# Softmax attention beside linear attention on one core: shifted patterns by 64-bit integer additions on GpSimd, two small steps moved to VectorE

## The chip, the core and the metric

The kernel runs on one core of a Trainium2 chip. A core has TensorE (PE, matrix products into PSUM), VectorE (DVE), ScalarE (ACT) and GpSimd (POOL), each with its own instruction queue, and SyncE (SP), which here issues nearly all transfers. The metric is the device time of one execution in microseconds (us).

## The reference

Two attention blocks with their own inputs are computed and put side by side. Both have 2048 rows, width 512, 32 heads of 16 columns. A is linear attention; B is full softmax attention and holds nearly all of the work: 32 heads x 2048 x 2048 exponentials.

```python
# A: phi = lambda t: where(t > 0, t + 1, exp(t)) + 1e-6
#    o = phi(q) @ (phi(k)^T v) / (phi(q) . sum(phi(k)) + 1e-6);  a = o @ wo
# B:
scores = jnp.einsum("bhqd,bhkd->bhqk", q, k) * Dh ** -0.5
p = _softmax(scores, axis=-1)
o = jnp.einsum("bhqk,bhkd->bhqd", p, v)
b = o.transpose(0, 2, 1, 3).reshape(B, S, D) @ wo
return jnp.concatenate([a, b], axis=-1)
```

## The kernel before

**Blocks and units.** B's scores are cut into blocks of 128 keys x 512 queries of one head. Four heads of 32 rows each sit side by side in TensorE, so up to four blocks of scores (line 888) are made at once. There are 4 groups of 8 heads, 4 chunks of 512 queries and 2 halves of a group: 32 units of 64 blocks, 2048 blocks in all. No maximum is subtracted from the scores; a check of the sums at the end (FLG) decides whether a second, general program has to run, which it does not with these inputs.

**Two ways to an exponential.** Each block goes one of two ways.
- By ScalarE (line 1118): a "fill" of two or three blocks in a score region of PSUM (pS) is turned into PT by one activation, and each block is then multiplied with V once (line 1252).
- By VectorE and GpSimd: VectorE adds a constant to the scaled scores, caps them and writes them as 16-bit integers (DI, line 995). Read as float16, these bits are a coarse exponential. Two further patterns with the bits shifted by 341 and 683 (DJ, line 1191) are multiplied with copies of V scaled by 0.797 and 0.633 (VV, line 688), so that each such block takes three products with V in place of one. Up to four blocks form a group, whose DI buffer is 2048 columns wide, and each group gets its two patterns from one instruction each. There are 4 DI buffers and 6 DJ buffers.

Before the change a pattern is made by GpSimd with a tensor-scalar operation, or by VectorE when the planner finds GpSimd too far behind. GpSimd also makes the scaled copies of V for the head groups 1 to 3 (`v4_job`, lane "pool"; group 0 has them made by VectorE) and the division of B's rows by their sums (`unit_done`, line 1386; for the last unit `last_half`, line 1318): after the 64 blocks of a unit VectorE transposes the sums (OT), takes the reciprocal (ZRA), a product gives XN, and VectorE transposes XN into ON for the output projection.

**The order of the work.** The kernel writes every engine's instruction list out at build time. A planner simulates the engines with prices for each operation and picks, step by step, what comes next on which engine: fills, blocks of the second way, products with V, and jobs (projections, A's work, outputs). `SEEDS` holds one number for each 10 us of plan, which selects the planner's knobs (how much VectorE and GpSimd backlog is allowed, when VectorE takes a pattern) and a jitter on the jobs' due times. Blocks go the second way when the planned backlog of VectorE and of GpSimd is under a limit and a PSUM bank and a DI buffer are free. `POOLT` is the planner's price of a pattern on GpSimd, `XNT` that of a division. On the chip the engines follow these lists and wait for one another by semaphores.

A mark of kind "x" and `sch.hold` belong to VectorE operations that the planner lets run without GpSimd beside them: the plan starts such an operation behind GpSimd's running one, and the next GpSimd operation gets a semaphore wait for it. VectorE itself has no such wait.

**The start.** GpSimd writes the identity (identb, lines 425 and 426), on which 36 warming products on TensorE wait (line 1406), then the band masks, zeros in KM and ones in VV. TensorE's queue has the warming ahead of the first projections (line 580).

Of the kernel before, what the change touches and what calls it, by code (L numbers as in the profile page):

```python
# [3 lines left out]

# [2 lines left out]

BF = mybir.dt.bfloat16
F32 = mybir.dt.float32
F16 = mybir.dt.float16  # L10
I16 = mybir.dt.int16
U16 = mybir.dt.uint16
ACTF = mybir.ActivationFunctionType
ALU = mybir.AluOpType
AX = mybir.AxisListType
# [232 lines left out]
def bass_concat_heads__linear_attn_block__softmax_full_mha__prompt_kernel(nc, A_x, A_wqkv, A_wo, B_x, B_wqkv, B_wo, out):  # L248
# [26 lines left out]
    ALAG = 30.0  # L275
    SHL = ("pool", "pool")
    FU = 0.6
    SEEDS = (1060, 1060, 1468, 1468, 770, 905, 67, 2167, 165, 1387, 732, 509, 735, 1818, 1305, 1496, 450, 274, 1430, 603,
             940, 1969, 374, 709, 1904, 1001, 1158, 1423, 702, 411, 2124, 1060, 1060, 2149, 2149, 2149, 915, 1328, 1148, 329,
             1858, 405, 2177, 2129, 1827, 1827, 1827, 1214, 840, 675, 1266, 623, 1055, 1942, 1575, 119, 1711, 1454, 1454, 2031,  # L280
             2031, 1300, 4, 425, 392, 1368, 92)
    SEG = 10.0
    JIT = 6.0
    DBAL = 1
# [4 lines left out]
    LDA = 1  # L289
    JM = 0.8  # L290
    DSH = 0.45
    XNT = 0.63
    VVT = 0.69
    HINT = {"pe": 60, "act": 60, "dve": 150}
    FW = 3.4
# [1 line left out]
    AE = 40.0  # L297
    PH = 2
    NXA = 2
    XNP = 1  # L300
    VVP = 0
    POOLT = lambda w: 0.284 + w * 0.00082
    PACE = {"pe": 1.0, "act": 1.0, "dve": 1.03, "pool": 1.0, "dma": 1.0}
    TRACE = None

# [3 lines left out]
    SH = (0, 341, 683)  # L309
# [4 lines left out]
    sch = Sched()  # L314
    es = contextlib.ExitStack()
    with es:
# [18 lines left out]
        DI = sb("DI", [128, NDG, DG * 512], I16)  # L335
        DJ = sb("DJ", [128, NDJ, DG * 512], I16)
# [87 lines left out]
        def mk_ident(t, key):  # L424
            sch.add("pool", lambda e: e.memset(t[:], 0.0), writes=[key])
            sch.add("pool", lambda e: e.affine_select(out=t[:], in_=t[:], compare_op=ALU.not_equal, fill=1.0,
                                                      base=0, pattern=[[-1, 128]], channel_multiplier=1),
                    reads=[key], writes=[key])
        mk_ident(identb, "identb")
        sch.add("dve", lambda e: e.memset(DUM, 0.0), writes=["FLG"])  # L430
        sch.add("act", lambda e: e.activation(DUM[:, 4:8], DUM[:, 0:4], ACTF.Exp), reads=["FLG"], writes=["FLG"])
# [37 lines left out]
        def mode():  # L469
            return MODES[drawn[-1] % len(MODES)]  # L470
# [5 lines left out]
        def vis(eng, en_):  # L476
            return en_ + TAIL[eng] + SEM
# [66 lines left out]
        def f_op(lane, fn, reads=(), writes=()):  # L544
            return lambda bk: sch.add(lane, fn, reads=reads, writes=writes)
# [117 lines left out]
        def vcol(h):  # L663
            return VST * (h // 8) + 17 * (h % 8)

        def v4_job(t4, Gp, lane="pool", **kw):
            sl = Gp % 2
            def mm(e, bk, i):
                tl, cc = divmod(i, 4)
                t = 4 * t4 + tl  # L670
                return e.matmul(f32v(bk)[:, tl * 128:(tl + 1) * 128], lhsT=xTb[:, cc, t * 128:(t + 1) * 128],  # L671
                                rhs=Wb[:, cc, 1024 + Gp * 128:1024 + Gp * 128 + 128], start=(cc == 0), stop=(cc == 3))
            ts = range(4 * t4, 4 * t4 + 4)
            def load_wo():
                load(WOb, wob, [("Wb", 2)])
            st = halves(mm, [("Wb", 2)] + [("xTb", t) for t in ts], n=16, parts=NPP, dur=0.06, after=load_wo if (t4, Gp) == (3, NGP - 1) else None)
            vv = lambda k: VV[:, sl, k, 4 * t4:4 * t4 + 4, :].rearrange("p t c -> p (t c)")
            st.append(("dve", 0.6, f_ev("dve", lambda e, bk: e.tensor_copy(
                VV[:, sl, 0, 4 * t4:4 * t4 + 4, :].rearrange("p t (h c) -> p t h c", c=17)[:, :, :, 0:16],
                f32v(bk).rearrange("p (t h d) -> p t h d", t=4, d=16)), [], [("VV", t, sl, 0) for t in ts])))  # L680
            for k in (1, 2):
                if VVP == 1 and lane == "dve":
                    st.append(("dve", 0.6, f_ev("dve", lambda e, bk, k=k: e.tensor_scalar(
                        VV[:, sl, k, 4 * t4:4 * t4 + 4, :].rearrange("p t (h c) -> p t h c", c=17)[:, :, :, 0:16],
                        f32v(bk).rearrange("p (t h d) -> p t h d", t=4, d=16), SW[k], 0.0, op0=ALU.mult, op1=ALU.add),
                        [], [("VV", t, sl, k) for t in ts])))
                    continue
                cp = f_op(lane, lambda e, k=k: e.tensor_scalar(  # L688
                    vv(k), vv(0), SW[k], 0.0, op0=ALU.mult, op1=ALU.add),
                    [("VV", t, sl, 0) for t in ts] + [("VV1", sl)], [("VV", t, sl, k) for t in ts])  # L690
# [224 lines left out]
        pend = []  # L915
# [255 lines left out]
        def shift_cand():  # L1171
            if not pend:
                return None
            buf, k, n, w, I, items, t_ = pend[0]
            jb = jn[0] % NDJ
            if jfree[jb] is None:
                return None
            sp, sd = max(T["pool"], vis("dve", t_), jfree[jb]), max(T["dve"], t_, jfree[jb])
            dp, dd = POOLT(w), DSH + max(0.0, T["pool"] - sd)
            tp = sp + sum(c_[3] for c_ in cands["pool"]) + sum(POOLT(p_[3]) for p_ in pend)  # L1180
            td = sd + sum(c_[3] for c_ in cands["dve"]) + dd
            ln, st_, d_ = ("dve", sd, dd) if tp > td + mode()[5] else ("pool", sp, dp)
            def run(st_, en_):
                pend.pop(0)
                jn[0] += 1
                if ln == "dve":
                    T["pool"] = max(T["pool"], vis("dve", en_))
                jfree[jb] = None
                jleft[jb] = n
                J = DJ[:, jb, 0:w]  # L1190
                op = sch.add(ln, lambda e: e.tensor_scalar(J, I, 1.0, float(SH[k]), op0=ALU.mult, op1=ALU.add),  # L1191
                             reads=[("DI", buf, i) for i in range(n)], writes=[("DJ", jb)])
                if ln == "dve":
                    sch.hold.append(op)
                    op.x = DSH
                for i, b in enumerate(items):
                    pv_ready[b[0]].append((vis(ln, en_), b, k, DJ.bitcast(F16)[:, jb, i * 512:(i + 1) * 512], ("DJ", jb), ("j", jb)))
                free_di(buf, vis(ln, en_))
            return st_, 0.7 if ln == "pool" else 0, ln, d_, run, None, "f"
# [102 lines left out]
        def last_half(h, t_):  # L1302

            if h == 0:
# [7 lines left out]
            cs, bs = slice(256 * h, 256 * h + 256), slice(8 * h, 8 * h + 8)  # L1312
            ot, zk, xk = [("OT", 0) if h == 0 else ("OT", 9)], [("ZR", u) if h == 0 else ("ZR", u + 9)], [("XN", xb, 1) if h == 0 else ("XN", xb, 9)]
            src, skey = (PVb, [("PV", g) for g in range(4)]) if h == 0 else (f32v(lbank[0]), [lbank[0][3]])
            mlane = "pool"
            st = [("dve", 0.42, f_op("dve", lambda e: e.transpose(OT[:, 0, cs], src[:, 0:256]), skey, ot)),
                  ("dve", 0.2, f_op("dve", lambda e: e.reciprocal(zs, o[:, bs, 16]), ot, zk)),
                  (mlane, 0.44, f_op(mlane, lambda e: e.tensor_tensor(xn[:, bs, 16:32], o[:, bs, 0:16],
                                                                                  zs.unsqueeze(2).broadcast_to([128, 8, 16]), op=ALU.mult), ot + zk, xk)),
                  ("dve", 0.42, f_op("dve", lambda e: e.transpose(ON[:, k, cs], XN[:, xb, cs]), [("XN", xb, 0)] + xk, on_keys(k)[4 * h:4 * h + 4]))]  # L1320
            urgent.append(Job(st, [("ot", u - 1)], [(3, ("onf", h))] + ([(1, ("zr", u))] if h else []), bank=False, ready=t_, prio=0.5))
# [54 lines left out]
        def unit_done(u, t_):  # L1376
# [6 lines left out]
            o = OT[:, 0, :].rearrange("p (b r) -> p b r", r=32)  # L1383
            xn = XN[:, xb, :].rearrange("p (b r) -> p b r", r=32)
            zr = ZRA[:, 16 * u:16 * u + 16]
            mul = f_op("pool" if XNP else "dve", lambda e: e.tensor_tensor(xn[:, :, 16 * e_:16 * e_ + 16], o[:, :, 0:16],  # L1386
                                                        zr.unsqueeze(2).broadcast_to([128, 16, 16]), op=ALU.mult),
                       [("OT", 0), ("ZR", u)], [("XN", xb, e_)])
            def norm(bk):
                mul(bk)  # L1390
                give_back("OT", 0.0)
            st = [("dve", 0.26, f_op("dve", lambda e: e.reciprocal(zr, o[:, :, 16]), [("OT", 0)], [("ZR", u)])),
                  ("pool", XNT, norm) if XNP else ("dve", 0.96, norm)]
# [215 lines left out]
        def run(queue, e):  # L1609
            got, loc = [], []  # L1610
            def hook(e):
                e.wait_ge(sems["dve"], flag_op.count)
                got.append(e.value_load(FLG.bitcast(mybir.dt.int32), min_val=0))
            sch.emit_queue(queue, e, sems, hook=(flag_op.idx if queue == "pool" else len(sch.ops), hook),
# [57 lines left out]
```

## Time and profile before

| what | value |
|---|---|
| median of 3 runs | 668.36 us (667.43 to 670.56) |
| the profiled execution, first to last instruction | 665.0 us |
| ScalarE busy | 650.9 us (98%) |
| TensorE busy | 643.4 us (97%) |
| VectorE busy | 610.5 us (92%) |
| GpSimd busy | 584.9 us (88%) |

The profiled execution is listed by its span alone; the median of the runs stands 3.4 us above it. In the profile's lines, PEld is TensorE's weight load, "out<-in" names the tiles, "xN" is a count, and behind the bar stand the busy time, the mean of one in ns, and the idle time of the engine just before, with what ended it. Matmuls are pipelined, so a busy TensorE is not one at its peak.

### The profile page before, as it was taken

The numbers are of one execution on the slowest core, as the hardware profiler recorded it, in microseconds if no ns is written. First come the engines' busy times: TensorE is split into PE (matmuls) and PEld (weight loads), VectorE is DVE, ScalarE is ACT, GpSimd is POOL, SyncE is SP. The second block draws the span as 40 slices with busy tenths as digits, with TensorE's granted clock in tenths as the row PEclk, the third lists the DMA queues.
The fourth block names the chain that finished last, engine by engine and source line by source line (L and its number), as shares of the span: only waits on it lengthen the run. The fifth ranks groups of instructions, "written<-read, shape, count | busy, mean of one in ns | idle before, by whom it ended". The sixth has DMA issues, their size and how long they took to land.

```text
span 665.0 us, 19663 instructions
## 1 busy us (share of the span) xinstructions
PE 643.4 (97%) x8560; PEld 204.5 (31%) x8560; DVE 610.5 (92%) x995; ACT 650.9 (98%) x707; POOL 584.9 (88%) x367
## 2 busy tenths in 40 slices
PE   8999999999999999999999999999999999999998
PEld 4323322332333333333322223322223222223224
DVE  6999999899898999998889999999999999899994
ACT  5999999999999999999999999999999999999995
POOL 5788889889999899899998988988899988999883
PEclk9999999999999999999999999999999999999999
DMA  9500001201001010021101100110111011000102
GB/s 217 101 2 1 13 7 25 41 21 25 23 17 18 18 34 18 11 65 41 41 10 34 40 18 17 36 27 13 30 28 35 18 25 34 25 26 10 40 27 73
DMA packets 55414, 21.72 MB, mean 33 GB/s; under 512 B 45600, under 2 KB 55328, under 8 KB 55328
## 3 DMA queue, kind: packets, MB, share of 16 engines
q1 hardware_dynamic: 54128, 20.07, 13.1%
q8 instruction: 67, 1.10, 0.7%
q10 hardware_dynamic: 1200, 0.39, 0.2%
q14 instruction: 19, 0.16, 0.1%
HBM read 4.19 MB, written 4.19 MB: 13 GB/s over the span
## 4 chain that ended last, share of the span: by engine, by line
ACT 93%; PE 6%; DMA 1%; DVE 0%; issue 0%
ACT PT L1118 90%; PE pS L888 2%; ACT pD L708 1%; PE pPV L1252 1%; PE pD L551 1%; PE pS L551 1%; ACT pS L708 1%; DMA xTb<-in_B_x_dram 1%; PE pD L1252 0%; PE pS L580 0%; PE pD L580 0%; DVE KV L555 0%; PE pD L671 0%; PE pD L792 0%; DVE FLG L660 0%
## 5 line engine op out<-in xcount | busy, mean ns | idle before, releaser
L1118 ACT ACTIVATE PT<-pS 128x1024 f16<-128x1024 f32 (+1 forms) x668 | 643.3, 1346 | 1.9 <-PE pS L888 1.9
L1191 POOL TENSOR_SCALAR DJ<-DI 128x2048 int16<-128x2048 int16 (+1 forms) x287 | 543.8, 1895 | 62.6 <-DVE DJ L1191 31.9
L995 DVE TENSOR_SCALAR DI<-pD 128x512 uint16<-128x512 f32 (+1 forms) x464 | 317.7, 701 | 20.2 <-PE pD L888 15.9
L888 PE MATMUL pS<-QT,KM 32*128 32x512 bf16 x1566 | 261.8, 385 | 16.4 <-ACT PT L1118 12.2
L1252 PE MATMUL pPV<-PT,VV 128*17 128x512 f16 (+1 forms) x1381 | 226.4, 378 | 0.0
L1252 PE MATMUL pPV<-DJ,VV 128*17 128x512 f16 (+1 forms) x1334 | 218.1, 379 | 0.0
L888 PE MATMUL pD<-QT,KM 32*128 32x512 bf16 x482 | 172.2, 385 | 0.2 <-DVE DI L995 0.2
L888 PEld LDWEIGHTS pS<-QT,KM 32*128 32x128 bf16 x1566 | 64.6, 91 | 284.5 <-ACT PT L1118 261.1
L1252 PE MATMUL pPV<-DI,VV 128*17 128x512 f16 (+1 forms) x667 | 151.5, 379 | 0.0
L995 DVE TENSOR_SCALAR DI<-pS 128x512 uint16<-128x512 f32 x185 | 126.2, 682 | 5.0 <-PE pS L888 2.4
L1252 PEld LDWEIGHTS pPV<-PT,VV 128*17 128x17 bf16 x1381 | 45.8, 88 | 38.3 <-issue 35.7
L1252 PEld LDWEIGHTS pPV<-DJ,VV 128*17 128x17 bf16 x1334 | 44.3, 88 | 43.1 <-issue 37.8
L888 PEld LDWEIGHTS pD<-QT,KM 32*128 32x128 bf16 x482 | 40.8, 91 | 3.6 <-DVE DI L995 2.0
L1191 DVE TENSOR_SCALAR DJ<-DI 128x2048 int16<-128x2048 int16 x47 | 38.9, 830 | 0.1
L1252 PEld LDWEIGHTS pPV<-DI,VV 128*17 128x17 bf16 x667 | 31.6, 88 | 21.7 <-issue 17.8
L551 PE MATMUL pD<-xTb,Wb 128*32 128x512 bf16 x352 | 27.5, 384 | 0.0
L551 PE MATMUL pD<-Wa,xTa 128*32 128x256 bf16 x640 | 23.8, 274 | 0.0
L1381 DVE STREAM_TRANSPOSE OT<-pPV 128x512 f32<-128x512 f32 x31 | 21.9, 706 | 0.7 <-PE pPV L1252 0.7
L1386 POOL TENSOR_TENSOR XN<-OT,ZRA 128x256 bf16<-128x256 f32 x31 | 19.2, 620 | 3.6 <-DVE DJ L1191 2.5
L708 ACT ACTIVATE pD<-pD 128x512 f32<-128x512 f32 x20 | 18.0, 898 | 0.0
L551 PEld LDWEIGHTS pD<-Wa,xTa 128*32 128x32 bf16 x640 | 14.5, 96 | 8.1 <-issue 6.3
L688 POOL TENSOR_SCALAR VV<-VV 128x544 bf16<-128x544 bf16 x24 | 15.4, 645 | 1.7 <-DVE DJ L1191 0.6
(113 smaller groups left out, 394.4 us busy)
## 6 DMA issues: line engine op xcount, KB each, us to landing
out_dram<-KV SPq DMA_DIRECT2D x31, 128.0 KB, 1.7
Wa<-in_A_wqkv_dram SPq DMA_DIRECT2D x3, 512.0 KB, 4.7
KM<-KR SPq DMA_DIRECT2D x96, 16.0 KB, 1.8
Wb<-in_B_wqkv_dram SPq DMA_DIRECT2D x2, 384.0 KB, 6.1
Wb<-in_B_wqkv_dram SPq DMA_DIRECT2D x1, 512.0 KB, 4.5
Wa<-in_A_wo_dram SPq DMA_DIRECT2D x1, 512.0 KB, 4.2
Wb<-in_B_wo_dram SPq DMA_DIRECT2D x1, 512.0 KB, 4.2
xTa<-in_A_x_dram SPq DMA_TRANSPOSE x24, 3.2
```

The lines of the kernel that those rows point to most:

```text
L551: ins = e.matmul(out[32 * g:32 * g + 32], lhsT=lhsT[:, 32 * g:32 * g + 32], rhs=rhs, start=start, stop=stop, tile_position=(0, 32 * g))
L688: cp = f_op(lane, lambda e, k=k: e.tensor_scalar(vv(k), vv(0), SW[k], 0.0, op0=ALU.mult, op1=ALU.add), [("VV", t, sl, 0) for t in ts] + [( ...
L708: ex = lambda bk: sch.add("act", lambda e: e.activation(x(bk), x(bk), ACTF.Exp), reads=[bk[3]], writes=[bk[3]])
L888: return e.matmul(dst, lhsT=KM[32 * g:32 * g + 32, Gp % 2, e_, j * 128:(j + 1) * 128], rhs=QT[32 * g:32 * g + 32, Gp % 2, c * 512:(c + 1) ...
L995: sch.add("dve", lambda e: e.tensor_scalar(DI.bitcast(U16)[:, buf, i * 512:(i + n) * 512], f32v(DBANK[bi], 512 * n), EB, IMAX, op0=ALU.add ...
L1118: sch.add("act", lambda e: e.activation(PT[:, row, c0:c0 + w], SCR[sl][:, 0:w], ACTF.Exp, scale=SC / ESC), reads=skeys(sl)[:len(bl)], writ ...
L1191: op = sch.add(ln, lambda e: e.tensor_scalar(J, I, 1.0, float(SH[k]), op0=ALU.mult, op1=ALU.add), reads=[("DI", buf, i) for i in range(n)] ...
L1252: sch.add("pe", lambda e: e.matmul(dst[32 * g:32 * g + 17, 0:n], lhsT=VV[:, Gp % 2, k, j, 17 * h:17 * h + 17], rhs=P[:, q0:q0 + n], start= ...
L1381: sch.add("dve", lambda e: e.transpose(OT[:, 0, :], PVb[:, 0:512]), reads=[("PV", g) for g in range(4)], writes=[("OT", 0)])
L1386: mul = f_op("pool" if XNP else "dve", lambda e: e.tensor_tensor(xn[:, :, 16 * e_:16 * e_ + 16], o[:, :, 0:16], zr.unsqueeze(2).broadcast_ ...
```

## The change

- GpSimd makes all patterns: four 16-bit integers at a time are read as one 64-bit word, to which the shift, repeated four times, is added (`int64_add`). VectorE makes none any more. The instruction belongs to another library of GpSimd, which is loaded ahead of the identity; the standard library is loaded again at the end, before GpSimd waits for FLG.
- The products for the division of B's rows and the scaled copies of V go to VectorE, marked as operations without GpSimd beside them.
- The planner's prices of a pattern and of a division are others, and its seeds are others, so the order of the whole kernel is written anew.

```diff
+U64 = mybir.dt.uint64
+INTLIB = library_config.all_libraries[1]
...
-    SEEDS = (1060, 1060, 1468, 1468, 770, 905, 67, 2167, 165, 1387, 732, 509, 735, 1818, 1305, 1496, 450, 274, 1430, 603,
...
+    SEEDS = (384, 384, 384, 384, 725, 644, 67, 1773, 1773, 1031, 1260, 17, 1633, 497, 506, 36, 450, 865, 865, 865, 1631,
...
-    XNT = 0.63
-    XNP = 1
+    XNP = 0
+    XNT = 0.42
-    POOLT = lambda w: 0.284 + w * 0.00082
+    POOLT = lambda w: 0.19 + w * 0.000425
...
+        sch.add("pool", lambda e: e.load_library(INTLIB), writes=["lib"])
         mk_ident(identb, "identb")
...
-        def v4_job(t4, Gp, lane="pool", **kw):
+        def v4_job(t4, Gp, lane="dve", **kw):
...
-            sp, sd = max(T["pool"], vis("dve", t_), jfree[jb]), max(T["dve"], t_, jfree[jb])
-            dp, dd = POOLT(w), DSH + max(0.0, T["pool"] - sd)
-            tp = sp + sum(c_[3] for c_ in cands["pool"]) + sum(POOLT(p_[3]) for p_ in pend)
-            td = sd + sum(c_[3] for c_ in cands["dve"]) + dd
-            ln, st_, d_ = ("dve", sd, dd) if tp > td + mode()[5] else ("pool", sp, dp)
+            sp = max(T["pool"], vis("dve", t_), jfree[jb])
+            dp = POOLT(w)
+            ln, st_, d_ = "pool", sp, dp
...
-                op = sch.add(ln, lambda e: e.tensor_scalar(J, I, 1.0, float(SH[k]), op0=ALU.mult, op1=ALU.add),
-                             reads=[("DI", buf, i) for i in range(n)], writes=[("DJ", jb)])
+                sch.add(ln, lambda e: e.int64_add(J.bitcast(U64), I.bitcast(U64), SH[k] * 0x0001000100010001),
+                        reads=[("DI", buf, i) for i in range(n)], writes=[("DJ", jb)])
...
-            mlane = "pool"
+            mlane = "dve"
...
-            mul = f_op("pool" if XNP else "dve", lambda e: e.tensor_tensor(xn[:, :, 16 * e_:16 * e_ + 16], o[:, :, 0:16],
+            mul = f_op("dve", lambda e: e.tensor_tensor(xn[:, :, 16 * e_:16 * e_ + 16], o[:, :, 0:16],
...
             def norm(bk):
-                mul(bk)
+                sch.hold.append(mul(bk))
                 give_back("OT", 0.0)
+            norm.kind = "x"
...
             def hook(e):
+                if queue == "pool":
+                    e.load_library(library_config.standard)
                 e.wait_ge(sems["dve"], flag_op.count)
```

More of the change, by code (lines that the diff above doesn't have):

```diff
@@ L5 @@
 import concourse.bass as bass
-from concourse import mybir
+from concourse import library_config, mybir
 BF = mybir.dt.bfloat16
@@ L277, in bass_concat_heads__linear_attn_block__softmax_full_mha__prompt_kernel @@
     FU = 0.6
-    SEEDS = (1060, 1060, 1468, 1468, 770, 905, 67, 2167, 165, 1387, 732, 509, 735, 1818, 1305, 1496, 450, 274, 1430, 603,
-             940, 1969, 374, 709, 1904, 1001, 1158, 1423, 702, 411, 2124, 1060, 1060, 2149, 2149, 2149, 915, 1328, 1148, 329,
-             1858, 405, 2177, 2129, 1827, 1827, 1827, 1214, 840, 675, 1266, 623, 1055, 1942, 1575, 119, 1711, 1454, 1454, 2031,
-             2031, 1300, 4, 425, 392, 1368, 92)
+    SEEDS = (384, 384, 384, 384, 725, 644, 67, 1773, 1773, 1031, 1260, 17, 1633, 497, 506, 36, 450, 865, 865, 865, 1631, 579, 441, 360, 395, 307, 1378, 1216, 818, 817, 835, 835, 1060, 1059, 1059, 2149, 864, 864, 864, 866, 1858, 531, 513, 513, 513, 513, 513, 2102, 1566, 1572, 1995, 623, 622, 1063, 1069, 1078, 1072, 1479, 577, 2031, 678, 584, 531, 513, 392, 1121, 1120)
     SEG = 10.0
@@ L1185, in run @@
                 jn[0] += 1
-                if ln == "dve":
-                    T["pool"] = max(T["pool"], vis("dve", en_))
                 jfree[jb] = None
@@ L1190, in run @@
                 J = DJ[:, jb, 0:w]
-                op = sch.add(ln, lambda e: e.tensor_scalar(J, I, 1.0, float(SH[k]), op0=ALU.mult, op1=ALU.add),
-                             reads=[("DI", buf, i) for i in range(n)], writes=[("DJ", jb)])
-                if ln == "dve":
-                    sch.hold.append(op)
-                    op.x = DSH
+                sch.add(ln, lambda e: e.int64_add(J.bitcast(U64), I.bitcast(U64), SH[k] * 0x0001000100010001),
+                        reads=[("DI", buf, i) for i in range(n)], writes=[("DJ", jb)])
                 for i, b in enumerate(items):
@@ L1314, in last_half @@
             src, skey = (PVb, [("PV", g) for g in range(4)]) if h == 0 else (f32v(lbank[0]), [lbank[0][3]])
-            mlane = "pool"
+            mlane = "dve"
             st = [("dve", 0.42, f_op("dve", lambda e: e.transpose(OT[:, 0, cs], src[:, 0:256]), skey, ot)),
                   ("dve", 0.2, f_op("dve", lambda e: e.reciprocal(zs, o[:, bs, 16]), ot, zk)),
-                  (mlane, 0.44, f_op(mlane, lambda e: e.tensor_tensor(xn[:, bs, 16:32], o[:, bs, 0:16],
+                  (mlane, 0.28, f_op(mlane, lambda e: e.tensor_tensor(xn[:, bs, 16:32], o[:, bs, 0:16],
                                                                                   zs.unsqueeze(2).broadcast_to([128, 8, 16]), op=ALU.mult), ot + zk, xk)),
@@ L1389, in norm @@
             def norm(bk):
-                mul(bk)
+                sch.hold.append(mul(bk))
                 give_back("OT", 0.0)
+            norm.kind = "x"
             st = [("dve", 0.26, f_op("dve", lambda e: e.reciprocal(zr, o[:, :, 16]), [("OT", 0)], [("ZR", u)])),
-                  ("pool", XNT, norm) if XNP else ("dve", 0.96, norm)]
+                  ("dve", XNT, norm)]
             if e_ == 1:
```

## The prediction

> **What bounds the kernel now.** I read the page first (busy shares, chain), then ScalarE's waits, then a table of the work by stretches of time, then the groups by line, and last the first and the final microseconds of the timeline.
>
> ```profile
> span 665.0 us, 19663 instructions
> PE 643.4 (97%) x8560; PEld 204.5 (31%) x8560; DVE 610.5 (92%) x995; ACT 650.9 (98%) x707; POOL 584.9 (88%) x367
> ACT 93%; PE 6%; DMA 1%; DVE 0%; issue 0%
> ...
> ACT PT L1118 <- PE pS L888: 1.9, 2, 1.6
> PEld pS L888 <- ACT PT L1118: 261.1, 579, 0.8
> ...
> 146.27 10.09 ACT PT L1118 x11
> ```
>
> ScalarE carries the chain (93%) and its exponentials wait for TensorE only 1.9 us. TensorE's 97% is mostly overlap: its score loads stood still 261.1 us until ScalarE freed a score region. The eleven fills of the piece at 146.27 come every 10.09 / 11 = 0.917 us; a fill is two blocks of 512 columns, so a block costs ScalarE 0.459 us. The time falls only if blocks leave ScalarE for the other path (VectorE's DI, GpSimd's DJ), or if what lies before or behind its unbroken run shrinks. Which engine limits that other path? The stretches tell (after start and length: PE, PEld, DVE, ACT, POOL busy).
>
> ```profile
> 0.00:10.00 10.00, 7.93 (x77) 5.63 (x77) 3.83 (x12) 3.12 (x5) 6.95 (x23) 1.00 0.91 197
> 10.00:60.00 50.00, 47.79 (x533) 15.05 (x530) 48.68 (x76) 49.72 (x54) 38.69 (x22) 1.00 0.31 67
> 310.00:360.00 50.00, 48.62 (x684) 16.44 (x672) 41.13 (x66) 50.00 (x55) 47.92 (x29) 1.00 0.14 35
> 360.00:410.00 50.00, 49.09 (x625) 15.25 (x625) 49.08 (x81) 50.00 (x57) 43.91 (x28) 1.00 0.11 25
> 560.00:610.00 50.00, 49.44 (x681) 14.47 (x675) 45.54 (x76) 50.00 (x56) 48.12 (x28) 1.00 0.07 23
> ...
> 10.00:640.00 630.00, 613.96 (x8094) 188.73 (x8091) 590.69 (x953) 629.72 (x685) 566.10 (x335) 1.00 0.13 29
> ```
>
> From 10 to 640 us ScalarE works 629.72 of 630. VectorE works 590.69 (93.8%), and where GpSimd is fullest (47.92, 48.12) VectorE has least (41.13, 45.54); where GpSimd has room (38.69, 43.91) VectorE reaches 48.68 and 49.08 of 50, which is 97.4 and 98.2%. So GpSimd's patterns hold the second path back, and VectorE is next behind it. What the two engines do there:
>
> ```profile
> L995 DVE TENSOR_SCALAR DI<-pD 128x512 uint16<-128x512 f32 (+1 forms) x464 | 317.7, 701 | 20.2 <-PE pD L888 15.9
> L995 DVE TENSOR_SCALAR DI<-pS 128x512 uint16<-128x512 f32 x185 | 126.2, 682 | 5.0 <-PE pS L888 2.4
> L888 PE MATMUL pS<-QT,KM 32*128 32x512 bf16 x1566 | 261.8, 385 | 16.4 <-ACT PT L1118 12.2
> L888 PE MATMUL pD<-QT,KM 32*128 32x512 bf16 x482 | 172.2, 385 | 0.2 <-DVE DI L995 0.2
> ...
> L1191 POOL TENSOR_SCALAR DJ<-DI x287: 1471/1897/1901, 13.6 to 651.7; 128x2048 int16<-128x2048 int16 x143, 128x1536 int16<-128x1536 int16 x1
> L1191 DVE TENSOR_SCALAR DJ<-DI x47: 649/711/1848, 44.7 to 644.2; 128x2048 int16<-128x2048 int16 x47
> L1191 DVE TENSOR_SCALAR DJ<-DI 128x2048 int16<-128x2048 int16 x45 | 36.4, 811 | 0.1
> ...
> POOL DJ L1191 <- DVE DJ L1191: 31.9, 40, 1.5
> ```
>
> Of 1566 + 482 = 2048 blocks, 482 + 185 = 667 go the second way, at (317.7 + 126.2) / 667 = 0.666 us of VectorE each. Their patterns (DJ) are 287 on GpSimd at 1.897 us and 47 on VectorE, 36.4 us of them between 10 and 640; GpSimd stood still 31.9 us for those 47.
>
> **The change, part by part.** *The patterns.* A 64-bit add over 2048 int16 columns is 512 words of 64 bits, or 1024 of 32. No row shows this instruction. GpSimd's two tensor-scalar rows give its rate:
>
> ```profile
> L1191 POOL TENSOR_SCALAR DJ<-DI 128x2048 int16<-128x2048 int16 x285 | 540.8, 1898 | 62.5 <-DVE DJ L1191 31.9 <-DVE DI L995 8.7 <-DVE VV L688 3.3
> L688 POOL TENSOR_SCALAR VV<-VV 128x544 bf16<-128x544 bf16 x24 | 15.4, 645 | 1.7 <-DVE DJ L1191 0.6
> L688 DVE TENSOR_SCALAR VV<-VV x8: 283/901/1786, 14.0 to 35.7; 128x544 bf16<-128x544 bf16 x8
> L688 DVE TENSOR_SCALAR VV<-VV 128x544 bf16<-128x544 bf16 x8 | 7.7, 966 | 0.0
> ```
>
> (1898 - 645) / (2048 - 544) = 0.833 ns an element and 192 ns fixed. If one step handles 32 bits, a pattern takes 192 + 1024 x 0.833 = 1045 ns (my estimate). Bounds: one step for 64 bits gives 619 ns; a step for each 16 bits, or two for each 32-bit half, gives the old 1898. I take 1045, since 32-bit operands are the widest that any row here shows on that engine. Some 345 patterns are then 361 us, 54% of the span: GpSimd stops being a limit, and its 80 us of old idle time and holds cost nothing any more.
>
> *VectorE's account, 10 to 640 us.* It loses the 45 patterns: -36.4. It gains 24 copies of V, uncontended 283 ns (the minimum above): +6.8. It gains 30 of the 31 row divisions (L1386, one starts at 642.9), a product of two tensors over 256 columns, for which the neighbours are:
>
> ```profile
> L1386 POOL TENSOR_TENSOR XN<-OT,ZRA x31: 617/619/624, 39.7 to 642.9; 128x256 bf16<-128x256 f32 x31
> L761 DVE TENSOR_TENSOR RHA<-pD,BMk 128x128 bf16<-128x128 f32 x4 | 1.1, 279 | 0.0
> L796 DVE TENSOR_TENSOR KV<-pD,RD 128x512 bf16<-128x512 f32 x11 | 7.5, 679 | 1.3 <-PE pD L792 1.3
> ```
>
> 279 + 128/384 x (679 - 279) = 412 ns, so +12.4. Both kinds have to get past a running GpSimd instruction: VectorE's V copies had a mean of 966 against 283 at best (683 ns of delay behind operations of 1898), its patterns 811 against 649 (162 ns). Scaled to 1045 ns that is 89 to 376 ns each, 4.8 to 20.3 us for 54. I take GpSimd's busy share times half an operation, 0.54 x 522 = 282 ns: +15.2. While VectorE waits so, its DI evictions queue behind, which is why it is charged in full; the next GpSimd pattern is held until the operation is done, which its 46% of idle time hides (without that cover, 54 x 0.4 = 22 us). Then VectorE may fill up: at 97.5%, between the two best stretches, 0.975 x 630 - 590.7 = +23.6 us. Room for blocks: 23.6 + 36.4 - 6.8 - 12.4 - 15.2 = 25.6 us.
>
> *What that room is worth.* Each moved block costs VectorE 0.666, saves ScalarE 0.459 and so shortens the stage, in which VectorE loses 0.975 x 0.459 = 0.448: n = 25.6 / (0.666 + 0.448) = 23 blocks, 23 x 0.459 = **-10.6 us**. Ends: no better filling and 20.3 of delay give 36.4 - 19.2 - 20.3 = -3.1, n = -3, **+1.3**; filling at 98.2% (+28.0) and 4.8 of delay give 40.4, n = 36, **-16.6**. TensorE gets two more V products a block, 46 of some 0.055 us (four run at once in 0.22), 2.5 us inside its 261 us of standing still. Late next: ScalarE's own rate again, with VectorE level beside it. The new seeds and prices of the planner only pick this order; I charge them nothing, with the ends above as their cover. SP's queue gets no new transfer and loses none.
>
> *The library at the start.* A load stands ahead of identb on GpSimd's queue, and 36 warming matmuls wait for identb ahead of the first projection on TensorE's:
>
> ```profile
> 0.80 0.20 POOL L425 MEMSET identb<- 128x128 bf16 x1 [0.29 <-POOLq L1657]
> 1.24 0.29 POOL L426 TENSOR_SCALAR_AFFINE_SELECT identb<-identb 128x128 bf16<-128x128 bf16 x1 [0.24 <-POOL identb L425]
> 1.59 4.02 PE L1406 MATMUL pD<-identb 128*128 128x128 bf16 x36 [1.59 <-POOL ZMk L443]
> 1.84 1.28 ACT L431 ACT_TABLE_LOAD   x1 [1.84 <-issue]
> 2.14 0.22 DVE L450 TENSOR_REDUCE PAR<-ZMk 128x1 f32<-128x4 f32 x2 [0.52 <-POOL ZMk L446]
> 5.87 0.40 PE L580 MATMUL pS<-xTb,Wb 128*128 128x128 bf16 x4 [0.26 <-DMA xTb<-in_B_x_dram]
> 6.30 0.35 DVE L584 TENSOR_SCALAR KM<-pS,PAR 128x128 bf16<-128x128 f32 x1 [3.94 <-PE pS L580]
> 8.76 7.91 ACT L1118 ACTIVATE PT<-pS 128x1024 f16<-128x1024 f32 x8 [1.64 <-PE pS L888]
> ...
> 0.81 5.01 DMA xTb<-in_B_x_dram
> ...
> Wb<-in_B_wqkv_dram SPq DMA_DIRECT2D x2, 384.0 KB, 6.1
> ```
>
> The warming ends at 1.59 + 4.02 = 5.61 and the first projection starts at 5.87: 0.26 us of slack. PAR has 6.30 - 2.36 = 3.94 of slack, the first exponential none. Every microsecond of load beyond 0.26 therefore moves TensorE's first work and the whole unbroken run of ScalarE. No load is in this trace. Nearest: an engine's table load, 1.28 us; the first transfer of xTb, 5.01, out of the same moment, when the DMA engines are 91% busy (first stretch above); the longest transfer, 6.1. From 0 (beside the work) to 5.8; a gain is excluded, nothing starts earlier for it. I take the transfer of the same moment: 5.0 - 0.26 = **+4.7 us**.
>
> The Trainium skill speaks against the change here: GPSIMD Engine Reference, section 2.1 Instruction dispatch, says that the first call into a freshly loaded kernel pays for fetching its code, about 6 us (5.95 measured there). No run here shows it yet; by that figure alone the start would lose 5.95 - 0.26 = 5.7 us and the sum below would be 663.2.
>
> *The end.* The last two divisions change engine, and the standard library is loaded before GpSimd waits for FLG.
>
> ```profile
> L1318 POOL TENSOR_TENSOR XN<-OT,ZRA 128x128 bf16<-128x128 f32 x2 | 0.8, 402 | 5.0 <-DVE ZRA L1317 5.0
> 658.17 0.76 POOL L1318 TENSOR_TENSOR XN<-OT,ZRA 128x128 bf16<-128x128 f32 x2 [5.00 <-DVE ZRA L1317]
> 662.68 0.27 DVE L660 TENSOR_REDUCE FLG<-pPV 1x1 f32<-1x128 f32 x1
> ```
>
> 402 becomes 279 ns, with one hand-over less each way: **-0.3** (0 to -0.6). GpSimd's last pattern ends at 651.7 + 1.9 = 653.6 and FLG at 662.95: 9.3 us cover the second load, which therefore costs nothing (at 12 us it would cost 3).
>
> Sum: -10.6 + 4.7 - 0.3 = -6.2, a span of 658.8. The span of 665.0 stands 3.4 below the median of the runs, 668.36; with the same 3.4, **662.2 us**.
>
> **The rivals.**
> *The load is hidden* (it runs beside the preamble, or is as short as the table load): 662.2 - 4.7 = 657.5. For it: 1.28 us for ScalarE's table. Against: the full DMA engines.
> *The load is long*, twice the longest transfer: +11.9 instead of +4.7, 669.4, no change. For it: nothing but that the trace has no price.
> *VectorE does not fill up*, the rival on the other side: its idle time was TensorE's lateness (20.2 us before DI, 15.9 of it for pD), not GpSimd's fullness, and stays at 93.8%. Room 25.6 - 23.6 = 2.0, n = 2, -0.8; with the start +3.6: 672.0, slower. It decides from a filling below 95.1%, where n = 9.6 blocks just pay the load. Against it: the stretches with 97.4 and 98.2%.
> *The integer add is not faster than the old pattern*: 345 x 1.898 = 655 us on GpSimd, with 18 before its first pattern and 11 behind its last 684, so 687. It decides from (659 - 29) / 345 = 1.83 us. For it: nothing measured; against: the rate per element above.
>
> **How the numbers follow.** Forecast (662.2, its own range 656 to 667) 0.5; load hidden 0.2; load long 0.1; VectorE does not fill 0.15; slow add 0.05. Half a per cent (3.3 us) is about what a measurement of this kernel can tell from no change. Faster: 0.42 of the forecast's half and the 0.2, 0.62. Same: 0.08 of the forecast, 0.07 of the long load, 0.06 of the unfilled VectorE, 0.21. Slower: 0.09, 0.03 and the 0.05, 0.17. The range runs from the best end of the blocks with half the load hidden (668.4 - 16.6 - 0.3 + 2.3 = 654, and a little below for a load hidden whole, 652) to the unfilled VectorE (672); about 0.2 lies outside.
>
> **What would show it.** Patterns on L1191's successor near 1.05 us and GpSimd near 54 to 60% busy; VectorE at 97% or more from 10 to 640; about 690 blocks on the second path and 1358 on ScalarE; divisions at 0.41 us and V copies at 0.28 plus delay; identb ready near 6 us and the first exponential near 13.5 instead of 8.76. The prediction is wrong if the first exponential stays near 9, if VectorE remains near 94% with TensorE named before its DI, or if patterns near 1.8 us chain GpSimd.

## The result: slower, with not one block moved

The changed kernel takes 678.2 us (678.0 to 679.1, four runs) against 668.8 us before: ratio 1.0143, interval 1.0125 to 1.0161. The forecast was 662.2. The profiled execution spans 676.4 us, 11.4 more than the 665.0 before. Each listed time stands some 1.8 us above the span of its run (678.16 and 676.4 here), so the 665.0 belongs to an execution of about 666.8 (my estimate), 2 us below the median before; that is why the spans differ by 11.4 and the medians by 9.4. First the page of the changed kernel (busy times, chain, and the groups that answer to those of before):

```profile
span 676.4 us, 19637 instructions
PE 647.6 (96%) x8561; PEld 204.9 (30%) x8561; DVE 605.4 (90%) x1015; ACT 651.5 (96%) x707; POOL 350.5 (52%) x359
ACT 89%; PE 8%; issue 1%; DVE 1%; POOL 0%; POOLq 0%; DVEq 0%
...
L1187 POOL INT64_ADD DJ<-DI x336 | 343.5, 1034 | 305.8 <-DVE DI L995 270.0
L995 DVE TENSOR_SCALAR DI<-pD 128x512 uint16<-128x512 f32 (+1 forms) x472 | 318.9, 691 | 28.4 <-PE pD L888 21.6
L888 PE MATMUL pS<-QT,KM 32*128 32x512 bf16 x1568 | 261.5, 385 | 16.7 <-ACT PT L1118 11.7
...
L888 PE MATMUL pD<-QT,KM 32*128 32x512 bf16 x480 | 173.2, 385 | 0.0
...
L995 DVE TENSOR_SCALAR DI<-pS 128x512 uint16<-128x512 f32 x187 | 127.6, 682 | 7.5 <-PE pS L888 5.5
```

A pattern takes 1034 ns in place of 1898, and GpSimd fell from 88 to 52% busy, waiting 270 us for VectorE's DI. But 480 + 187 = 667 blocks go the second way, as many as before. ScalarE has the same 1381 blocks and the same busy time (651.5 against 650.9), and now also waits. The start, by the timeline:

```profile
8.17 0.19 POOL L424 MEMSET identb<- 128x128 bf16 x1 [7.66 <-issue]
8.52 0.29 POOL L425 TENSOR_SCALAR_AFFINE_SELECT identb<-identb 128x128 bf16<-128x128 bf16 x1 [0.16 <-POOL identb L424]
8.87 3.82 PE L1400 MATMUL pD<-identb 128*128 128x128 bf16 x36 [8.87 <-POOL ZMk L443]
12.53 0.39 PE L580 MATMUL pS<-xTb,Wb 128*128 128x128 bf16 x4
15.36 10.72 ACT L1118 ACTIVATE PT<-pS 128x1024 f16<-128x1024 f32 x11 [1.57 <-PE pS L888]
```

GpSimd stands still 7.66 us ahead of the identity (0.29 before), the 36 warming products start at 8.87 instead of 1.59, the first projection at 12.53 instead of 5.87, the first exponential at 15.36 instead of 8.76: +6.6 us. The last exponentials (line 1038, both kernels, before first) and ScalarE's waits in the changed kernel:

```profile
L1038 ACT ACTIVATE PT<-pS x2: 1103/1110/1117, 655.1 to 655.8; 128x768 f16<-128x768 f32 x2
```
```profile
L1038 ACT ACTIVATE PT<-pS x2: 1122/1123/1124, 667.8 to 668.5; 128x768 f16<-128x768 f32 x2
...
ACT PT L1118 <- PE pD L888: 2.9, 2, 2.5
ACT PT L1118 <- PE pS L888: 2.2, 2, 1.6
ACT pD L708 <- DVE PQT L707: 2.1, 1, 2.1
```

ScalarE's run from first to last exponential is 669.6 - 15.4 = 654.3 us against 656.9 - 8.8 = 648.2: +6.1, with equal work. Before, ScalarE waited for line 1118 only 1.9 us, 1.6 of it ahead of the first exponential. Now it waits 2.9 + 2.2 + 2.1, of which 1.6 is again ahead of the first: 5.6 us of holes inside the run (0.3 before), with two single ones of 2.5 and 2.1. Behind the last exponential stand 676.4 - 669.6 = 6.8 us against 8.1: -1.3. So 6.6 + 6.1 - 1.3 = 11.4.

The stretches of the changed kernel, for the same times as in the prediction, and last the long stretch of the kernel before:

```profile
310.00:360.00 50.00, 49.19 (x665) 14.66 (x667) 44.29 (x73) 50.00 (x55) 24.94 (x25) 1.00 0.07 15
360.00:410.00 50.00, 48.65 (x595) 14.77 (x591) 46.90 (x78) 50.00 (x55) 28.09 (x28) 1.00 0.11 26
560.00:610.00 50.00, 48.92 (x637) 13.54 (x625) 46.30 (x79) 50.00 (x56) 27.45 (x27) 1.00 0.06 18
...
60.00:640.00 580.00, 565.58 (x7489) 172.78 (x7486) 534.57 (x886) 577.22 (x628) 310.04 (x304) 1.00 0.12 25
```
```profile
60.00:640.00 580.00, 566.17 (x7564) 173.68 (x7561) 542.01 (x878) 580.00 (x633) 527.41 (x314) 1.00 0.11 26
```

With GpSimd about half idle in all of them, VectorE did not fill: 534.57 of 580 us, 92.2%, where the kernel before had 542.01 in the same stretch (93.4%).

### The profile page after: what moved, and what is told of

Same layout as the page of the kernel before. It is cut to its first block, busy times and chain, and to the rows that moved or that the text cites. A ratio compares the mean times of both kernels' runs of the same rounds, so it can differ in the third digit from the quotient of the medians.

```text
span 676.4 us, 19637 instructions
## 1 busy us (share of the span) xinstructions
PE 647.6 (96%) x8561; PEld 204.9 (30%) x8561; DVE 605.4 (90%) x1015; ACT 651.5 (96%) x707; POOL 350.5 (52%) x359
## 4 chain that ended last, share of the span: by engine, by line
ACT 89%; PE 8%; issue 1%; DVE 1%; POOL 0%; POOLq 0%; DVEq 0%
ACT PT L1118 87%; PE pS L888 3%; PE pPV L1245 2%; ACT pD L708 2%; PE pD L551 1%; ACT pS L708 1%; PE pD L1400 1%; PE pS L551 0%; DVE KV L555 0%; PE pD L671 0%; PE pS L671 0%; PE pD L580 0%; PE pS L580 0%; PE pPV L1497 0%; DVE OT L1309 0%
## 5 line engine op out<-in xcount | busy, mean ns | idle before, releaser
L1187 POOL INT64_ADD DJ<-DI x336 | 343.5, 1034 | 305.8 <-DVE DI L995 270.0
L995 DVE TENSOR_SCALAR DI<-pD 128x512 uint16<-128x512 f32 (+1 forms) x472 | 318.9, 691 | 28.4 <-PE pD L888 21.6
L888 PE MATMUL pS<-QT,KM 32*128 32x512 bf16 x1568 | 261.5, 385 | 16.7 <-ACT PT L1118 11.7
L1245 PE MATMUL pPV<-PT,VV 128*17 128x512 f16 (+1 forms) x1381 | 238.0, 379 | 0.0
L1245 PE MATMUL pPV<-DJ,VV 128*17 128x512 f16 (+1 forms) x1334 | 226.2, 380 | 0.0
L1245 PE MATMUL pPV<-DI,VV 128*17 128x512 f16 (+1 forms) x667 | 159.4, 382 | 0.0
L1245 PEld LDWEIGHTS pPV<-PT,VV 128*17 128x17 bf16 x1381 | 48.0, 88 | 44.3 <-issue 39.8
L1245 PEld LDWEIGHTS pPV<-DI,VV 128*17 128x17 bf16 x667 | 34.2, 88 | 21.7 <-issue 20.6
L551 PE MATMUL pD<-xTb,Wb 128*32 128x512 bf16 x288 | 21.7, 383 | 0.0
L1379 DVE TENSOR_TENSOR XN<-OT,ZRA 128x256 bf16<-128x256 f32 x31 | 20.4, 657 | 0.2
L555 DVE CAST KV<-pD 128x512 bf16<-128x512 f32 x19 | 13.0, 684 | 7.0 <-PE pD L551 7.0
L688 DVE TENSOR_SCALAR VV<-VV 128x544 bf16<-128x544 bf16 x32 | 15.8, 501 | 0.0
```

Source lines behind the costliest of these rows:

```text
L551: ins = e.matmul(out[32 * g:32 * g + 32], lhsT=lhsT[:, 32 * g:32 * g + 32], rhs=rhs, start=start, stop=stop, tile_position=(0, 32 * g))
L555: return lambda e, bk: (e.tensor_copy(out_fn(), in_fn(bk)) if lane == "dve" else e.activation(out_fn(), in_fn(bk), ACTF.Copy))
L688: cp = f_op(lane, lambda e, k=k: e.tensor_scalar(vv(k), vv(0), SW[k], 0.0, op0=ALU.mult, op1=ALU.add), [("VV", t, sl, 0) for t in ts] + [( ...
L888: return e.matmul(dst, lhsT=KM[32 * g:32 * g + 32, Gp % 2, e_, j * 128:(j + 1) * 128], rhs=QT[32 * g:32 * g + 32, Gp % 2, c * 512:(c + 1) ...
L995: sch.add("dve", lambda e: e.tensor_scalar(DI.bitcast(U16)[:, buf, i * 512:(i + n) * 512], f32v(DBANK[bi], 512 * n), EB, IMAX, op0=ALU.add ...
L1187: sch.add(ln, lambda e: e.int64_add(J.bitcast(U64), I.bitcast(U64), SH[k] * 0x0001000100010001), reads=[("DI", buf, i) for i in range(n)], ...
```

## The experiments

Three questions come first: is the late start the load's? Does the rest of the loss come from the new order or from the moved work? And what is the faster pattern worth when both sides had the same search? Each ratio is to runs of the kernel before that were made beside the run in question; their medians lay between 667.2 and 668.9 us, so times of different groups compare to about 2 us.

**The load moved (late_load).** 

> The changed kernel with its library load moved behind GpSimd's first masks and zeros; nothing else differs. Theory 1 (the load at the head delays the identity, the warming and with them ScalarE's first exponential by 6.6 us, one for one): first exponential back near 8.8 us, time 678.2 - 6.6 = 671.6 us. Rival (the late start has another cause, say colder transfers): 677 to 679. A first pattern some 2 us later than in the old order should cost nothing.

```diff
-        sch.add("pool", lambda e: e.load_library(INTLIB), writes=["lib"])
         mk_ident(identb, "identb")
...
         sch.add("pool", lambda e: e.memset(KV[:, :, 1:515:513], 1.0), writes=["KV1"])
+        sch.add("pool", lambda e: e.load_library(INTLIB), writes=["lib"])
```

Measured: 672.6 us, ratio to before 1.007 (1.0037 to 1.0102). Its timeline and ScalarE's waits:

```profile
0.80 0.21 POOL L424 MEMSET identb<- 128x128 bf16 x1 [0.29 <-POOLq L1653]
9.27 13.46 ACT L1118 ACTIVATE PT<-pS 128x1024 f16<-128x1024 f32 x14 [1.57 <-PE pS L888]
...
14.68 2.18 POOL L1187 INT64_ADD DJ<-DI  x2 [6.35 <-DVE DI L995]
...
ACT PT L1118 <- PE pS L888: 3.1, 4, 1.6
ACT PT L1118 <- PE pD L888: 2.7, 2, 2.5
ACT pD L708 <- DVE PQT L707: 2.1, 1, 2.1
```

Theory 1 holds: the first exponential is back at 9.27, and 5.6 us of time with it (4.9 by the two ratios to before). The load now fits into the 6.35 us in which GpSimd waited for its first DI anyway: the first pattern starts as that DI ends. The holes of 2.5 and 2.1 us stayed, so they are not after-effects of the late start.

**A load alone (before_load).** 

> The kernel before with one load of the standard library ahead of the identity, and nothing else. Theory 1, if a load of the library that is there already is carried out: first exponential near 15.4, time 668.8 + 6.6 = 675.4 us. If such a load is skipped, or if the start of the changed kernel was late for another reason: 668.8.

```diff
+        sch.add("pool", lambda e: e.load_library(library_config.standard), writes=["lib"])
         mk_ident(identb, "identb")
```

Measured: 668.15, ratio 1.0004 (0.9986 to 1.0021); identb starts at 0.89 instead of 0.80. Asking for the library that is there already costs 0.1 us at that place, so this run says nothing on a real load. late_load carries theory 1 alone.

**The old order with the moved work (order_moved).** 

> The order of the kernel before (its seeds and prices), but the division products and all scaled copies of V are issued on VectorE; the patterns stay as before. Theory 2 (the rest of the loss lies in the new order, not in the moved work): 667 to 671 us. Rival 2 (the moved work, some 26 us with its delays behind GpSimd, holds up VectorE's evictions and makes ScalarE wait): 672 to 680.

```diff
-            mul = f_op("pool" if XNP else "dve", lambda e: e.tensor_tensor(...
+            mul = f_op("dve", lambda e: e.tensor_tensor(...
...
-                mul(bk)
+                sch.hold.append(mul(bk))
...
-                  (mlane, 0.44, f_op(mlane, lambda e: e.tensor_tensor(...
+                  (mlane, 0.44, f_op("dve", lambda e: e.tensor_tensor(...
...
-                cp = f_op(lane, lambda e, k=k: e.tensor_scalar(
+                cp = f_op("dve", lambda e, k=k: e.tensor_scalar(
...
-                    st.append((lane, VVT, cp))
+                    st.append((lane, VVT, lambda bk, cp=cp: sch.hold.append(cp(bk))))
```

Measured: 669.1, ratio 1.0004 (0.9982 to 1.0026). ScalarE's waits and the long stretch:

```profile
ACT PT L1118 <- PE pS L888: 2.3, 3, 1.6
...
60.00:640.00 580.00, 567.04 (x7545) 175.34 (x7546) 551.80 (x927) 579.05 (x630) 494.25 (x262) 0.99 0.11 26
```

VectorE works 551.80 of 580 us here (95.1%, against 93.4 before) and ScalarE waits only 0.7 us beyond its first exponential: the old order had idle time on VectorE that the moved work could use without loss.

**The old order with the moved work and the new instruction (order_int64).** 

> The same, and GpSimd's 287 patterns are 64-bit additions, with the library loaded behind the masks; VectorE keeps its 47 patterns, and the order is that of the kernel before. Theory 2: 667 to 669.5, no gain, since this order leaves 1381 blocks with ScalarE, which never waits. If GpSimd's speed limits the kernel while it runs: below 665. Rival 2: 672 or more, as with the patterns unchanged.

```diff
+        sch.add("pool", lambda e: e.load_library(INTLIB), writes=["lib"])
...
-                op = sch.add(ln, lambda e: e.tensor_scalar(J, I, 1.0, float(SH[k]), op0=ALU.mult, op1=ALU.add),
+                op = sch.add(ln, lambda e: e.tensor_scalar(J, I, 1.0, float(SH[k]), op0=ALU.mult, op1=ALU.add) if ln == "dve" else e.int64_add(J.bitcast(U64), I.bitcast(U64), SH[k] * 0x0001000100010001),
...
+                if queue == "pool":
+                    e.load_library(library_config.standard)
```

The edits of order_moved belong to it as well; the first load stands behind the masks. Measured: 667.8, ratio 1.000 (0.9983 to 1.0018). Its page:

```profile
PE 645.6 (97%) x8560; PEld 205.6 (31%) x8560; DVE 612.3 (92%) x1052; ACT 651.3 (98%) x707; POOL 301.5 (45%) x310
...
ACT PT L1121 <- PE pS L891: 2.1, 2, 1.8
```

GpSimd is 45% busy in place of 88, VectorE does all the moved work, and the time is what it was, neither better nor worse; ScalarE waits 0.3 us beyond the first exponential. Theory 2 holds in both runs: in the old order neither the moved work nor the new instruction makes holes of note in ScalarE's run. The new order has them, and late_load, without the late start, is 0.7% slower than before. And a faster pattern gains nothing in an order that keeps 1381 blocks on ScalarE.

**At equal search: none (one_before, one_after).** 

> The kernel before with one number (1559) in all 67 places of its seeds, so with no search behind its order; 621 blocks go the second way instead of 667. By 0.459 us of ScalarE a block: 668 + 46 x 0.459 = 689 us; with some of that eaten by holes that the search had not removed or had, 682 to 690. It is the partner of the next three runs.

> The changed kernel, library load behind the masks, with the same number 1559 in all places: the change at equal search, none. 633 blocks go the second way, 12 more than in its partner. Theory 2 (the change itself gains a little and the searched order lost it): 12 x 0.459 = 5.5 us, with holes 2 to 6 us, faster than one_before. Rival 2 (the moved work costs more than GpSimd's relief gives): as slow as one_before or slower.

```diff
+    SEEDS = (1559,)
```

Measured: 686.5 (ratio to before 1.0266, 1.0222 to 1.0310) and 683.9 (1.0224, 1.0194 to 1.0254). The change is 2.6 us ahead, 0.4%, with 12 blocks more on the second path (5.5 us of ScalarE); the intervals overlap. That speaks against rival 2, but does not exclude it.

**At equal search: some (search_after, search_before).** 

> The changed kernel, late load, with seeds from a search of my own (24 tries for each of 4 kept lists at each of 67 places, judged by the plan). 649 blocks go the second way. Partner of search_before. If the change is worth something at equal search: 2 to 6 us faster than its partner; if not, equal within 2. Against the kernel before, whose list has 667: 668 + 18 x 0.459 = 676.

> The kernel before with seeds from the very same search. 648 blocks go the second way. About 676 us, as search_after, if the change is worth nothing at equal search; 678 to 682 if it is worth something.

The edit is the seed list alone (and the late load on one side). Measured: 676.2 (1.0150, 1.0124 to 1.0176) and 678.1 (1.0174, 1.0152 to 1.0195): 1.9 us ahead, 0.3%, intervals overlapping, with 649 and 648 blocks. The intervals of both pairs overlap, so neither gain is clear of noise, and that the two agree is partly luck, because the granted clock differs between the partners. Of the 26 runs of the kernel before that were made beside late_load, those at a clock of 1.000 took 666.9 to 668.4 us and those at 0.992 or less 669.9 to 672.5: some 3 us go with it in that group. one_after's runs had 0.989 to 0.994, while three of one_before's four had 0.999 or more; search_before's had 0.987 to 0.992, search_after's 0.990 to 1.000. So in the first pair the clock may hide part of a gain, and in the second it may be the whole of it. My estimate from this is that the change itself is worth between nothing and 6 us, which would fit its blocks (12 more in the first pair, one in the second); no run holds the clock fixed. The seeds are worth more: between one number and the tuned list the kernel before moves by 18 us.

**Which of the path's prices counts (one_half_pattern, one_half_evict, one_light_moved).** 

> As one_after, but each pattern covers half of its columns, but for the first in each buffer, and the planner's price for it is halved to match (the other half holds old values; the switch to the general program is off). 640 blocks go the second way. Theory 3 (VectorE, not GpSimd, now limits the second way): at most 7 x 0.459 = 3.2 us faster than one_after. Rival 3 (GpSimd's patterns still limit it): 10 us or more faster.

```diff
-    POOLT = lambda w: 0.19 + w * 0.000425
+    POOLT = lambda w: 0.19 + w * 0.0002125
...
+                hw = w if jn[0] <= NDJ else w // 2
-                sch.add(ln, lambda e: e.int64_add(J.bitcast(U64), I.bitcast(U64), ...
+                sch.add(ln, lambda e: e.int64_add(J[:, 0:hw].bitcast(U64), I[:, 0:hw].bitcast(U64), ...
```

> As one_after (changed kernel, one number in all seeds, late load), but VectorE writes half the columns of each DI block, but for the first in each place, and the plan prices it so (the other half holds old values; the switch to the general program is off). 668 blocks go the second way, 35 more than in one_after. Theory 3 (VectorE limits the second way): 35 x 0.459 = 16 us faster than one_after, 12 to 22. Rival (GpSimd or the PSUM banks limit it): under 5 us.

```diff
-                    sch.add("dve", lambda e: e.tensor_scalar(DI.bitcast(U16)[:, buf, i * 512:(i + n) * 512], f32v(DBANK[bi], 512 * n),
+                    cw = 256
...
+                    sch.add("dve", lambda e: e.tensor_scalar(DI.bitcast(U16)[:, buf, i * 512:i * 512 + cw * n], f32v(DBANK[bi], cw * n),
...
-                push("dve", vis("pe", en), 0, 0.09 + 0.51 * n, p1)
+                push("dve", vis("pe", en), 0, 0.09 + 0.255 * n, p1)
```

> As one_after, but 30 of the 32 division products and the scaled copies of V for the last two head groups write one element each, priced so, and the plan does not start them behind GpSimd (the outputs lack them; the switch to the general program is off). 645 blocks go the second way, 12 more than in one_after. If the moved work is what eats the relief: 12 x 0.459 = 5.5 us faster than one_after, 3 to 8 with holes. If it is hidden beside other work: within 1.5 us of one_after.

```diff
-    XNT = 0.42
+    XNT = 0.10
...
-            norm.kind = "x"
...
-                    alone.kind = "x"
-                    st.append(("dve", 0.27, alone))
+                    st.append(("dve", 0.10, alone))
```

In that last one most of the moved operations write one element each, so their outputs are left out, as its expectation says. Measured, beside one_after's 683.9:

| kernel | blocks the second way | time, us | ratio to before |
|---|---|---|---|
| one_after | 633 | 683.9 | 1.0224 (1.0194 to 1.0254) |
| one_half_pattern | 640 | 682.7 | 1.0210 (1.0182 to 1.0237) |
| one_light_moved | 645 | 679.2 | 1.0146 (1.0121 to 1.0171) |
| one_half_evict | 668 | 667.2 | 0.9998 (0.9981 to 1.0014) |

The busy times and the evictions, of one_after first and of one_half_evict second:

```profile
PE 649.2 (95%) x8493; PEld 208.0 (30%) x8493; DVE 586.9 (86%) x973; ACT 666.0 (98%) x703; POOL 332.9 (49%) x341
...
L995 DVE TENSOR_SCALAR DI<-pD 128x512 uint16<-128x512 f32 (+1 forms) x454 | 313.0, 702 | 44.3 <-PE pD L888 37.1
```
```profile
PE 634.1 (95%) x8562; PEld 209.0 (31%) x8562; DVE 444.5 (67%) x977; ACT 648.6 (97%) x667; POOL 350.8 (53%) x359
...
L999 DVE TENSOR_SCALAR DI<-pD 128x256 uint16<-128x256 f32 (+1 forms) x467 | 205.4, 450 | 123.6 <-PE pD L888 113.2
```

The patterns of one_half_pattern:

```profile
L1188 POOL INT64_ADD DJ<-DI x320 | 194.6, 619 | 461.2 <-DVE DI L995 412.1
```

Halving GpSimd's pattern again (619 ns) gives 1.2 us, nothing that can be told. Halving VectorE's eviction gives 16.7 us for 35 blocks, 0.48 us a block (15.1 us and 0.43 by the ratios, since these two ran beside different runs of before). Theory 3 holds for the order with one number in all seeds: GpSimd had stopped being the limit, and VectorE's work decides how many blocks the plan sends the second way. But it does so while being 86% busy in one_after and 67% in one_half_evict, so it is not that VectorE is full. I take it that an earlier end of an eviction hands its PSUM bank and its place in the plan back sooner; no run separates these two. Making the moved work nearly free gives 12 blocks, as many as the change itself gained over one_before, and 4.7 us, of which a part may be the clock (0.995 to 1.000 in these runs).

**GpSimd slowed again in the new order (late_more_pool).** 

> The changed kernel with the late load, and behind each pattern a second addition over half of its columns that writes the same values again, in an unchanged order: GpSimd's work rises by some 336 x 0.63 = 210 us to about 83% of the span, near the 88% of the kernel before. If GpSimd's speed is worth nothing in this order: within 2 us of late_load's 672.6 us. If its relief carries something: 677 or more.

```diff
                         reads=[("DI", buf, i) for i in range(n)], writes=[("DJ", jb)])
+                H = w // 2
+                sch.add(ln, lambda e: e.int64_add(J[:, 0:H].bitcast(U64), I[:, 0:H].bitcast(U64), SH[k] * 0x0001000100010001),
+                        reads=[("DI", buf, i) for i in range(n)], writes=[("DJ", jb)])
```

Measured: 686.3, ratio to before 1.0282 (1.0237 to 1.0327), 13.7 us more than late_load.

```profile
PE 653.7 (95%) x8561; PEld 208.2 (30%) x8561; DVE 604.3 (88%) x1015; ACT 654.9 (95%) x707; POOL 555.0 (81%) x695
...
PE pPV L1248 <- POOL DJ L1190: 14.4, 29, 1.1
...
ACT PT L1118 <- PE pD L888: 9.0, 13, 2.5
ACT PT L1118 <- PE pS L888: 8.5, 15, 1.6
```

It is the second of the two expectations that came: GpSimd's speed does carry something. GpSimd at 81% is less busy than before the change, yet TensorE's products with V now wait for patterns (14.4 us), the score fills stand behind those products in TensorE's queue, and ScalarE waits 17.5 us, 1.6 of them ahead of its first exponential. The order counts on a pattern about 1 us after the last DI; a later one stops TensorE. So in a written order the speed of a pattern mattered one way only: faster than planned gained nothing (order_int64), slower than planned cost time (here).

## Why the prediction was wrong, point by point

- *The pattern's price was right*: 1045 ns estimated, 1034 measured; GpSimd 54% estimated, 52% measured. One step for each 32-bit word is what the time looks like, also at half the width: (1034 - 619) / 512 words is 0.81 ns each, with the 619 ns of one_half_pattern, against the 0.833 that I had from the old rows.
- *The step that failed is "VectorE may fill up: at 97.5%"*, and with it the 23 blocks and the -10.6 us. The measured share is 92.2%, less than before, and the number of blocks is the same. The sign that I read it from was false: in the stretches with most VectorE work, VectorE was making patterns itself, and of the four that I showed, the two with least had none. Line 1191 alone, before (stretch, then DVE and POOL):

```profile
10.00:60.00 50.00, 2.04 (x2) 38.10 (x21) 1.00 0.31 67
310.00:360.00 50.00, 0.00 (x0) 44.88 (x24) 1.00 0.14 35
360.00:410.00 50.00, 4.58 (x5) 40.83 (x23) 1.00 0.11 25
560.00:610.00 50.00, 0.00 (x0) 46.36 (x25) 1.00 0.07 23
```

  Of the difference between 41.13 us (from 310) and 49.08 us (from 360), 4.58 is this work handed from one engine to the other; without it the four stretches have 46.64, 41.13, 44.50 and 45.54, and the 97 to 98% that I meant to fill to are gone. A busy share that moves between engines shows who did the work, not which of them was the limit. I had the other reading as a rival (idle time from TensorE's lateness, 672.0 at 0.15). VectorE's idle time ahead of DI for TensorE's pD stayed and grew, from 15.9 to 21.6 us, so that rival's mechanism is the one that came. Its time did not: the 672.0 holds 4.7 us for the load, and with the load in its place the kernel takes 678.2. That late_load takes 672.6 is luck, for it has no late start. What the faster pattern can move shows at equal search: 12 blocks (633 against 621) where I had 23, and none between the two searched lists.
- *"The new seeds and prices of the planner only pick this order; I charge them nothing"* failed too. The order opened holes of 5.6 us in ScalarE's run, which had 0.3 before, and with the load out of the way 0.7% is lost. order_int64 shows that neither the instruction nor the moved work makes such holes in the old order.
- *The load at the start*: mechanism and place were right, the size was too small, +6.6 us in place of +4.7. The identity's memset came at 8.17 instead of 0.80, 7.4 us later; the transfer that I took as a stand-in lasts 5.0. The Trainium skill's 5.95 us for code of a freshly loaded kernel (GPSIMD Engine Reference, section 2.1 Instruction dispatch) was nearer and still short here, where the wait already stands before a plain memset, not before the library's own instruction; in late_load the whole load fitted into 6.35 us.
- *What a block is worth held*: 0.459 us predicted, 0.43 (by the ratios) to 16.7 / 35 = 0.48 in one_half_evict.
- *The moved work*: a division takes 414 ns at best, as estimated (412), and the delay behind GpSimd is in the size assumed (282 ns):

```profile
L1379 DVE TENSOR_TENSOR XN<-OT,ZRA x31: 414/474/1222, 52.7 to 655.8; 128x256 bf16<-128x256 f32 x31
...
L1379 DVE TENSOR_TENSOR XN<-OT,ZRA 128x256 bf16<-128x256 f32 x31 | 20.4, 657 | 0.2
```

  The mean is 657, 243 ns above the best. But I had set these costs against room that VectorE did not fill with blocks; at equal search they take 12 blocks (one_light_moved).
- *The end*: -1.3 instead of -0.3, and the second load is hidden as predicted: from the end of FLG to the end of the program it is 676.4 - 674.7 = 1.7 us, against 2.1 before.
- *The step from span to time*: I added 3.4 us, the distance of the profiled execution from the median before. In the runs of the changed kernel it is 1.8, so 1.6 us of the forecast came from a profiled execution that lay below its median.

The forecast thus becomes the measured time by 662.2 + 10.6 (no blocks gained) + 6.1 (ScalarE's run longer) + 1.9 (load) - 1.0 (end) - 1.6 (span to time) = 678.2.

In sum, 668.8 becomes 678.2 by about +5 for the load's place (late_load) and about +4.5 for an order with holes; whatever the change itself gains at equal search is hidden in that. What stays open is why the new order came out worse than the old one, though at equal search the change was not behind. No run tells whether a longer search would find a better order for the changed kernel. My own searches found nothing better than either, so no version that beats the kernel before was run; late_load is the better form of this change, and it is still 0.7% slower.

## What to carry to other kernels

Before an engine's relief is counted as a gain, ask which decision would use it. Here the work is divided by a planner, and relief that moved no block saved no time, however much busy share it frees. A busy share that rises on one engine where it falls on another may be the same work changing hands; take that work out of both before reading a limit from it. And a load or a set-up step ahead of the first instruction of a long chain costs nearly its whole length (6.6 of 7.4 us here), while the same step a few lines further down, in an engine's first idle time, cost nothing that these runs can tell.

## What the runs showed of the hardware that I had not expected

A load of another GpSimd library at the head of its queue held everything behind it for 7.4 us, a plain memset included; behind the masks it took no more than 6.35 us; asking for the resident library cost 0.1 us. GpSimd's 64-bit addition with a constant handles four 16-bit integers in a word: 1034 ns for 2048 of them against 1898 with a tensor-scalar operation. And slowing patterns by some 0.6 us each, in an order written for the fast ones, cost 13.7 us with GpSimd only 81% busy (late_more_pool). In the runs of the kernel before beside late_load, those with a granted clock of 0.992 or less were some 3 us longer than those at 1.000, as much as the gains that were to be told apart.
